# Summing the weighted values of a windowed attention with 32x32 in place of 64x64 identity blocks

## The chip, the cores and the metric

The kernel runs on one core of a Trainium2 chip. The metric is device time in microseconds (us) of one execution, the median of several runs. PE is TensorE (matmuls), PEld its weight loads, DVE is VectorE, ACT is ScalarE, POOL is GpSimd and SP is SyncE, which here only issues transfers. All line numbers (L739) are those of the kernel before.

## The reference

Two independent halves share the inputs' length of S = 2048 tokens and D = 576 channels, and their results stand side by side in the output. Half A is an attention with 32 heads of 18 channels, in which a token sees 8 earlier tokens at a distance of 0, 2, ... 14. Half B is a long convolution. Cut to what matters:

```python
def A(x, wqkv, wo):                  # H = 32, Dh = 18, W = 8, dil = 2
    q, k, v = split(x @ wqkv)
    logits[h, s, w] = q[h, s] . k[h, s - 2 * w] * Dh ** -0.5
    attn = softmax(logits, axis=w)
    o[h, s] = sum_w attn[h, s, w] * v[h, s - 2 * w]      # the change is in this sum
    return o @ wo

def B(q, k, v, shift_k, ssm_k, ssm_D):
    kv = shift(k, shift_k) * v
    return q * (causal_conv(kv, ssm_k) + kv * ssm_D)     # by transforms, written as matmuls

out = concat([A, B], axis=-1)
```

## The kernel before

**Layout.** Half A keeps channels on partitions and time along the free dimension. The 576 channels are four tiles of 128 and one half tile of 64, which is folded so that two halves of the time fill 128 partitions. Time comes in four blocks of 512, each in two halves of 256 (`hh`). A *chunk* `(hh, c)` holds two time blocks for `c` = 0 or 1 (the full tiles), and the folded tile for `c` = 2: six chunks in all.

**Stages.** First come the projections (L310 to L346), the filter spectra of half B (L515 to L530), then the logits (L624, L633), the softmax (L644 to L668), and then the stage of the change, `weigh` (L713 to L758), about 118 to 164 us. Afterwards half B's products (L860), their sums (`ps_z`, L880), the inverse transforms (`ps_inv`, L912, `ps_back`, L953) and the output projection of half A (`ps_wo`, L792) follow.

**weigh.** For a chunk, `spread` (L694) has sent the attention weights to a tile X with each weight repeated for its channels. For a channel tile, DVE multiplies X by the values, shifted by 2, 4, ... 16 places (L723): one instruction of 4096 elements per partition, laid out as two time blocks x 8 window places x 256 tokens. The products P go to three buffers in turn: two wide tiles and a part of `qk`. The sum over the 8 window places is made on PE: matmuls with blocks of the identity matrix as weights, accumulated in PSUM. For `c` < 2 two channel tiles P0 and P1 are summed together (L735 to L741): for each window place, four matmuls of 64x64 with 512 columns, one for each pair of source half and tile. The half `h` of the rows goes to bank `h` and to the half `(h + s) % 2` of the partitions, so that the four use four different blocks of the array. ACT then copies the two banks to `pv` in one instruction (L743). There are eight such sums, four for each `hh`, and two for the folded tile (L753, 256 columns, copied by L757), each of which stands right behind the last of the four.

**Output weights.** As the sum turns one half of the channels, the rows of `wo` are loaded in the order in which the channels lie in `pv` (L765 to L773, on POOL's queue).

**What sets the order.** The program's order is fixed when it is built; at run time each engine works through its list. Between the steps, `until()` (L282) takes as many pieces of independent work from a list `units` as the table `PLACES` says: projections of the values (`ps_proj`), the spectra of half B's input (`ps_fx`, L586, copied by L589), and in the second half the output projection (`ps_wo`, copied by L799). They are put ahead of a sum on PE. A small bookkeeping of clocks (`clk`, `psum`, L258) decides which unit of the inverse transforms is taken in the last stage; the count of pieces doesn't depend on it.

**PSUM.** The pool has two tags, A and B, with two buffers of two banks each (`bank2`, L88). Each request takes the next buffer of its tag, and its first writer waits until the last reader of what was in there is done. `ps_proj`, `ps_wo`, `ps_inv` and `ps_back` use A; the sums (`ps_acc`), the logits and `ps_z` use B; the units of `ps_fx` take B and A in turn (L581), the odd ones B.

Of the kernel before, what the change touches and what calls it, by code (L numbers as in the profile page):

```python
# [11 lines left out]
ACT = mybir.ActivationFunctionType  # L12
# [12 lines left out]
def view(t, offset, dims):  # L25

    return bass.AP(tensor=t.tensor, offset=t.offset + offset, ap=[list(t.ap[0])] + [list(d) for d in dims])
# [3 lines left out]
def kernel(  # L31
# [13 lines left out]
    nc = tc.nc  # L45
    Bsz, S, D = A_x.shape
    assert Bsz == 1 and S == 2048 and D == 576
    H, DH, W, DIL = 32, 18, 8, 2
# [39 lines left out]
    def bank2(name, tag):  # L88
        return pp.tile([128, 2, 512], FP32, name=name, tag=tag)
# [126 lines left out]
    ident = main.tile([128, 128], BF16, name="ident")  # L216
# [18 lines left out]
    for c0, p0, p1 in ((0, 0, 128), (128, 0, 128), (256, 0, 128), (384, 0, 128), (512, 0, 64), (512, 64, 128)):  # L235
        EHS.append(main.tile([128, 32], BF16, name=f"E{len(EHS)}"))
        e = EHS[-1][p0:p1, :]
# [20 lines left out]
    clk = {"D": 0.0, "P": 0.0, "A": 0.0}  # L258
    psum = {"A": deque([0.0, 0.0]), "B": deque([0.0, 0.0])}

    def dve(n, fn, ready=0.0, ns=0.53):

        fn()
        clk["D"] = max(clk["D"], ready) + n * ns / 1000 + 0.125
        return clk["D"]

    def pe(us, tag, evac, ready=0.0, first=True, last=True):

        clk["P"] = max(clk["P"], ready, psum[tag].popleft() if first else 0.0) + us
        clk["A"] = max(clk["A"], clk["P"] + 0.1) + evac  # L270
        if last:
            psum[tag].append(clk["A"])
        return clk["A"]
# [8 lines left out]
    def until():  # L282

        for _ in range(next(places, 0)):
            if units:
                p = max(clk["P"], psum["A"][0] if psum["A"] else 0.0)
                pop(next((n for n, u in enumerate(units) if len(u) < 4 or u[3] <= p), 0))

    def need(label):
        while any(u[2] == label for u in units):  # L290
            pop()
# [141 lines left out]
    for n0 in range(0, D, 256):  # L433
        n = min(256, D - n0)
        ps = bank2("ps_sk", "A" if n == 256 else "B")
        for h in range(0, n, 128):
            w = min(128, n - h)
            sk = skrow[:, 4 * (n0 + h):4 * (n0 + h + w)].rearrange("p (d j) -> p d j", j=4)
            for r in range(2):
                nc.tensor.matmul(ps[64 * r:64 * r + 64, h // 128, 0:4 * w], onesb[:, 0:64],  # L440
                                 sk if r else view(skrow, 4 * (n0 + h) + 3, [[4, w], [-1, 4]]),
                                 start=True, stop=True, tile_position=(0, 64 * r))
# [36 lines left out]
    def taps(i):  # L479
        kj, vt = kjs[i], vts[i]  # L480
        kv = ab[:, i].rearrange("p s c d -> p (s c) d")
        for j in (3, 2, 1, 0):
            o = kv if j == 3 else sp1.tile([128, 4, D], BF16, name="tB")[:]
            dve(2304, lambda: nc.vector.tensor_tensor(  # L484
                o, kj[:, 3 - j:7 - j, :], skb[:, 3 - j, :].unsqueeze(1).to_broadcast([128, 4, D]), ALU.mult))
            if j < 3:
                dve(2304, lambda: nc.vector.tensor_tensor(kv, kv, o, ALU.add))  # L487
        return dve(2304, lambda: nc.vector.tensor_tensor(kv, kv, vt[:], ALU.mult))
# [57 lines left out]
    for i in range(NBL):  # L546
        r = taps(i)
# [51 lines left out]
    for jj, i in ((0, 0), (1, 2)):  # L599
# [6 lines left out]
        for n in range(2):  # L606
            a, b = last[4 * n:4 * n + 4], rest[4 * n:4 * n + 4]
# [4 lines left out]
    def wide(name):  # L612
        return sv.tile([128, 4096], BF16, name=name, tag="prod", bufs=2)
# [69 lines left out]
    pv = main.tile([128, 9216], BF16, name="pv", tag="r_ktok")  # L683
# [29 lines left out]
    def weigh(n):  # L713

        hh, c = chunks[n]
        X = Xt[n]

        def product(ct):
            need(f"v{c}{ct}")
            voff = ct * KW + (1024 * c if ct < 4 else 0)  # L720
            P = qk[:, 8192:12288] if nP[0] % 3 == 2 else wide("P")[:]
            nP[0] += 1
            r = dve(4096, lambda: nc.vector.tensor_tensor(  # L723
                view(P, 0, [[2048, 2], [256, W], [1, 256]]), view(X, 0, [[2048, 2], [256, W], [1, 256]]),
                view(v, voff + 2 + 256 * hh, [[512, 2], [2, W], [1, 256]]), ALU.mult))
            return P, r

        if c < 2:
            for cp in range(2):
                P0, _ = product(2 * cp)  # L730
                yield
                P1, r = product(2 * cp + 1)
                until()
                acc = bank2("ps_acc", "B")
                for u in range(W):  # L735
                    for s, P in enumerate((P0, P1)):
                        for h in range(2):
                            o = (h + s) % 2
                            nc.tensor.matmul(acc[64 * o:64 * o + 64, h, :], ident[64 * h:64 * h + 64, 64 * h:64 * h + 64],  # L739
                                             view(P, 256 * u, [[2048, 2], [1, 256]])[64 * h:64 * h + 64],  # L740
                                             start=(u == 0), stop=(u == W - 1), tile_position=(64 * h, 64 * o))  # L741
                pe(1.9, "B", 1.02, r)
                nc.scalar.activation(view(pv, 4608 * hh + 2048 * c + 1024 * cp, [[512, 2], [1, 512]]), acc[:], ACT.Copy)  # L743
                yield
        else:
            P, r = product(4)
            until()
            acc = bank2("ps_acc", "B")
            for u in range(W):
                for s in range(2):  # L750
                    for h in range(2):
                        o = (h + s) % 2
                        nc.tensor.matmul(acc[64 * o:64 * o + 64, h, 0:256], ident[64 * h:64 * h + 64, 64 * h:64 * h + 64],  # L753
                                         view(P, 2048 * s + 256 * u, [[1, 256]])[64 * h:64 * h + 64],
                                         start=(u == 0), stop=(u == W - 1), tile_position=(64 * h, 64 * o))
            pe(1.0, "B", 0.6, r)
            nc.scalar.activation(view(pv, 4608 * hh + 4096, [[256, 2], [1, 256]]), acc[:, :, 0:256], ACT.Copy)  # L757
            yield  # L758
# [5 lines left out]

    wo = view(qk, 12288, [[2 * D, 2], [D, 2], [1, D]])  # L765
    woh = view(qk, 12288 + 4 * D, [[1, D]])
    for e in range(2):
        for b in range(2):
            nc.gpsimd.dma_start(wo[64 * e:64 * e + 64, :, b, :],
                                bass.AP(tensor=A_wo.tensor, offset=A_wo.offset + ((0, 3), (2, 1))[e][b] * D,  # L770
                                        ap=[[9 * D, 64], [4 * D, 2], [1, D]]))
        nc.gpsimd.dma_start(woh[64 * e:64 * e + 64, :],
                            bass.AP(tensor=A_wo.tensor, offset=A_wo.offset + 8 * D, ap=[[9 * D, 64], [1, D]]))  # L773
    nst = [0]
# [31 lines left out]
    def outputs(hh):  # L806
        for j in range(2):
            for sb in (2 * hh, 2 * hh + 1):
                for h in range(2):
                    units.append((1.15, partial(output, j, sb, h), "wo"))  # L810

    pvs = (None for n in range(len(chunks)) for _ in weigh(n))
    steps(pvs, 1)
    steps(sb_, 1)
# [50 lines left out]
    acc = {}  # L865

    def sums(j, t, i, pr, ready):

        until()
        sc, ss = CSG[j - i], SSG[j - i]  # L870
        for r, terms in enumerate((((0, 0, sc), (1, 1, ss)), ((1, 0, sc), (0, 1, -ss)))):
            if i == 0:
                acc[r] = bank2("ps_z", "B")
                clk["P"] = max(clk["P"], psum["B"][r])
            for n, (part, cs, sign) in enumerate(terms):
                w = ident if sign > 0 else identn
                for s in range(2):
                    for h in range(2):
                        o = 64 * ((h + s) % 2)
                        nc.tensor.matmul(view(acc[r], 512 * h, [[192, 2], [96, 2], [1, 96]])[o:o + 64], w[64 * h:64 * h + 64, 64 * h:64 * h + 64],  # L880
                                         pr[64 * h:64 * h + 64, part, cs, :].rearrange(
                                             "p (a g e) -> p g a e", a=2, g=4)[:, 2 * s:2 * s + 2],
                                         start=(i == 0 and n == 0), stop=(i == j and n == 1),
                                         tile_position=(64 * h, o))
            clk["P"] = max(clk["P"], ready) + 0.34
        if i == j:
            for r in range(2):
                y, z = (view(Yall, (j % 2) * 8 * D + r * 4 * D + TH * t, [[2 * D, 2], [D, 2], [1, TH]]),
                        view(acc[r], 0, [[512, 2], [TH, 2], [1, TH]]))
                if (j, t, r) == (NBL - 1, 2, 1):  # L890
                    nc.vector.tensor_copy(y, z)
                else:
                    nc.scalar.activation(y, z, ACT.Copy)  # L893
                out = pe(0.0, "B", 0.85)
            return out
# [102 lines left out]
    for n, (j, t, i) in enumerate(todo):  # L998
# [3 lines left out]
        r = sums(j, t, i, *prs.pop(n))  # L1002
        new = []
        if i == j and t == 2 and j < NBL - 1:
            a, b = inverse(j, 0, HD, r), inverse(j, HD, HD, r)
# [40 lines left out]
```

## Time and profile before

| what | us |
|---|---|
| median of 3 runs (224.27 to 224.85) | 224.3 |
| the profiled execution | 225.0 |
| its span on the core | 223.0 |
| PE busy, share of the span | 213.1, 96% |
| DVE busy | 208.1, 93% |
| ACT busy | 154.4, 69% |
| granted TensorE clock | full throughout |

"Busy" counts the time in which at least one instruction of the engine runs; matmuls overlap, so a busy PE isn't a PE at its peak. A group's row gives the line, engine and operation, what it writes and reads, the shape, the count, its busy time and the mean of one, then the idle time of the engine before it and what ended that. A row of the timeline gives the start and the length in us, and a group may hold several instructions of one line in a row. A row of the windows gives the length of the stretch, the busy time of PE, PEld, DVE, ACT and POOL, each with its count, then the granted clock, the share of the transfer engines and GB/s.

### The profile page before, as it was taken

To read this page: it belongs to the slowest core of one execution; us is meant where nothing else is said; L and a number is where in the kernel's file an instruction comes from. 1 tells how busy PE (TensorE), PEld (TensorE's weight loads), DVE (VectorE), ACT (ScalarE), POOL (GpSimd) and SP (SyncE) were. 2 spreads that over 40 slices of the span, in tenths; PEclk is the share of its full clock that TensorE was granted. 3 is DMA by queue.
4 is the path that set the end of the run, shared out by engine and by line. 5 is a ranking of instruction groups with operands and counts; after the bars stand their busy time and mean duration, and the time that the engine had idled before them with its cause. 6 is when DMAs were issued, how large, how long until landed. Compare 5 with 4: busy or idle time off the path is not lost.

```text
span 223.0 us, 5309 instructions
## 1 busy us (share of the span) xinstructions
PE 213.1 (96%) x2271; PEld 118.2 (53%) x2271; DVE 208.1 (93%) x156; ACT 154.4 (69%) x213; POOL 31.9 (14%) x68
## 2 busy tenths in 40 slices
PE   7999999999999999999999999999999999999891
PEld 2543444444566556753444445665656667666560
DVE  7789999999988999999899999999999899999992
ACT  5858766888596987756667768885678887655630
POOL 8860000000000040403410000015000000330000
PEclk9999999999999999999999999999999999999999
DMA  5999999999900047659999469917211103662016
GB/s 187 274 229 219 188 241 203 221 207 235 216 0 0 3 83 131 117 95 169 198 190 235 124 114 203 225 32 234 88 56 53 57 3 107 199 208 75 3 53 159
DMA packets 30985, 31.41 MB, mean 141 GB/s; under 512 B 16849, under 2 KB 26705, under 8 KB 30962
## 3 DMA queue, kind: packets, MB, share of 16 engines
q1 hardware_dynamic: 25714, 21.93, 44.6%
q0 software_dynamic: 2624, 6.64, 14.6%
q10 hardware_dynamic: 2624, 2.51, 3.3%
q8 instruction: 17, 0.28, 0.5%
q14 instruction: 6, 0.05, 0.1%
HBM read 13.11 MB, written 4.72 MB: 80 GB/s over the span
## 4 chain that ended last, share of the span: by engine, by line
PE 76%; DVE 9%; ACT 5%; issue 4%; DMA 3%; SPq 1%; DVEq 0%; ACTq 0%
PE ps_proj L310 15%; PE ps_fk L515 10%; PE ps_wo L792 7%; PE ps_fx L586 6%; DVE qk L860 6%; PE ps_z L880 5%; PE ps_log L633 5%; PE ps_fk L516 5%; PE ps_acc L739 4%; PE ps_inv L912 4%; PE ps_proj L427 3%; PE ps_proj L315 3%; DMA X<-attn 3%; PE ps_proj L322 3%; PE ps_idle L138 2%
## 5 line engine op out<-in xcount | busy, mean ns | idle before, releaser
L860 DVE TENSOR_TENSOR qk<-xw,Ks 128x3072 bf16<-128x3072 bf16 x30 | 50.5, 1750 | 1.2 <-PE ps_z L880 1.0
L624 DVE TENSOR_TENSOR prod<-qk 128x4096 bf16<-128x4096 bf16 (+1 forms) x20 | 40.6, 2074 | 3.4 <-PE ps_log L633 3.3
L310 PE MATMUL ps_proj<-xw 128*128 128x512 bf16 x160 | 38.4, 380 | 0.0
L515 PE MATMUL ps_fk<-kTok,TK 128*128 128x384 bf16 x128 | 32.8, 327 | 0.6 <-ACT Ks L530 0.5
L516 PE MATMUL ps_fk<-kTok,TK 128*128 128x192 bf16 x128 | 31.4, 246 | 0.0
L530 ACT ACTIVATE Ks<-ps_fk 128x576 bf16<-128x576 f32 x32 | 20.4, 653 | 9.9 <-PE ps_fk L516 9.7
L310 PEld LDWEIGHTS <-xw 128*128 128x128 bf16 x160 | 14.3, 98 | 18.9 <-issue 4.9
L893 ACT ACTIVATE Yall<-ps_z 128x768 bf16<-128x768 f32 x23 | 17.4, 808 | 6.1 <-PE ps_z L880 5.9
L346 ACT ACTIVATE qk<-ps_proj 128x1024 bf16<-128x1024 f32 x14 | 14.4, 1027 | 7.1 <-PE ps_proj L310 3.4
L589 ACT ACTIVATE xw<-ps_fx 128x576 bf16<-128x576 f32 x32 | 18.6, 660 | 0.2
L515 PEld LDWEIGHTS <-TK 128*128 128x128 bf16 x128 | 12.5, 98 | 11.8 <-issue 4.2
L792 PE MATMUL ps_wo<-qk,pv 128*128 128x288 bf16 x128 | 17.9, 287 | 0.0
L586 PE MATMUL ps_fx<-ab,TX 64*128 64x288 bf16 x256 | 17.7, 283 | 0.0
L487 DVE TENSOR_TENSOR ab<-ab,tB 128x2304 bf16<-128x2304 bf16 x12 | 16.3, 1358 | 0.4
L880 PE MATMUL ps_z<-qk,ident 64*64 64x384 bf16 x288 | 16.4, 325 | 0.3 <-ACT pv L743 0.3
L484 DVE TENSOR_TENSOR tB<-kj,skb 128x2304 bf16<-128x2304 bf16 x12 | 16.3, 1356 | 0.3
L912 PE MATMUL ps_inv<-Yall,TI 128*128 128x288 bf16 (+1 forms) x112 | 15.5, 292 | 0.7 <-ACT Yall L893 0.6
L739 PE MATMUL ps_acc<-P,ident 64*64 64x512 bf16 x192 | 15.3, 379 | 0.0
L346 ACT ACTIVATE v<-ps_proj 128x1024 bf16<-128x1024 f32 x9 | 9.2, 1022 | 8.8 <-PE ps_proj L322 4.6
L586 PEld LDWEIGHTS <-TX 64*128 64x128 bf16 x256 | 11.7, 94 | 6.5 <-issue 3.6
L799 ACT ACTIVATE qk<-ps_wo 128x576 bf16<-128x576 f32 x16 | 10.4, 651 | 6.1 <-PE ps_wo L792 3.0
L792 PEld LDWEIGHTS <-pv 128*128 128x128 bf16 x128 | 11.5, 98 | 6.0 <-issue 3.2
(146 smaller groups left out, 352.8 us busy)
## 6 DMA issues: line engine op xcount, KB each, us to landing
kj<-in_B_k_dram SPq DMA_DIRECT2D x7, 504.0 KB, 8.1
Ks<-Ks POOLq DMA_DIRECT2D x6, 576.0 KB, 7.7
qk<-attn SPq DMA_DIRECT2D x12, 256.0 KB, 5.8
vt<-in_B_v_dram SPq DMA_DIRECT2D x8, 288.0 KB, 8.6
out_dram<-qk ACTq DMA_DIRECT2D x8, 288.0 KB, 2.9
X<-attn SPq DMA_DIRECT2D x8, 256.0 KB, 5.1
Ks<-in_A_x_dram SPq DMA_DIRECT2D x2, 576.0 KB, 5.2
xw<-in_A_wqkv_dram SPq DMA_DIRECT2D x2, 576.0 KB, 7.4
```

The source lines that it names most:

```text
L310: nc.tensor.matmul(ps[:, jp, :], wq(kb, comp, 128 * ct, 128), xT(kb, 1024 * jj + 512 * jp, 512), start=(kb == 0 and not first), stop=(kb = ...
L346: nc.scalar.activation(view(t, o + pad + 1024 * jj, [[512, 2], [1, 512]]), ps[:], ACT.Copy)
L515: nc.tensor.matmul(o[:, 0:2], w, rhs[:, 0:2], start=start, stop=stop)
L516: nc.tensor.matmul(o[:, 2], w, rhs[:, 2], start=start, stop=stop)
L530: nc.scalar.activation(view(Ks, (3 - m) * SPB + 4 * D * cs + 96 * gi, [[768, 3], [384, 2], [1, 96]]), acc3(ps), ACT.Copy, scale=(CSG, SSG) ...
L586: nc.tensor.matmul(ps[:, pm, 0:HD], TX[64 * pm:64 * pm + 64, c, 128 * gi:128 * gi + 128], kv[64 * pm:64 * pm + 64, c, HD * h:HD * h + HD], ...
L624: r = dve(1024 * nj, lambda: nc.vector.tensor_tensor(view(prod, 0, [[256 * nj, 4], [256, nj], [1, 256]]), view(t, o + 256 * hh, [[0, 4], [ ...
L739: nc.tensor.matmul(acc[64 * o:64 * o + 64, h, :], ident[64 * h:64 * h + 64, 64 * h:64 * h + 64], view(P, 256 * u, [[2048, 2], [1, 256]])[6 ...
L792: nc.tensor.matmul(ps[:, r, 0:HD], oT(hh, j + 2 * r, t)[:, o:o + 128], wo[:, t // 2, t % 2, HD * h:HD * h + HD], start=(t == 0 and h == 0) ...
L860: r = dve(3072, lambda: nc.vector.tensor_tensor(pr, view(xw, i * SPB + 4 * TH * t, [[4 * D, 2], [0, 2], [1, 4 * TH]]), view(Ks, (3 - j + i ...
L880: nc.tensor.matmul(view(acc[r], 512 * h, [[192, 2], [96, 2], [1, 96]])[o:o + 64], w[64 * h:64 * h + 64, 64 * h:64 * h + 64], pr[64 * h:64 ...
L912: nc.tensor.matmul(ps[:, c, 0:n], TI[:, sl, pm, 128 * c:128 * c + 128], Yall[:, j % 2, pm, sl, c0:c0 + n], start=(pm == 0 and sl == 0), st ...
```

## The change

For `c` < 2 the sum is made with 32x32 blocks of the identity: for each window place sixteen matmuls of 256 columns, for the two channel tiles `p`, the two time blocks `jj` and the four groups `g` of 32 rows. The group goes to the partitions `32 * ((g + p + 2 * jj) % 4)`, and each pair `(p, jj)` has a PSUM bank of its own, so that a sum takes four banks: both buffers of tag B. ACT copies them out in three instructions: the first time block's two banks (128 partitions), and the second time block's in two pieces of 64 partitions, which swap the halves of the partitions so that both time blocks lie alike in `pv`. As the second channel tile of a pair is turned by 32 partitions there, the rows of the output weights are loaded in five pieces in place of four. The folded tile's sum stays as it was. The bookkeeping of clocks gets the new figures.

```diff
@@ weigh, c < 2
-                acc = bank2("ps_acc", "B")
+                acc = [bank2("ps_acc", "B") for _ in range(2)]
                 for u in range(W):
-                    for s, P in enumerate((P0, P1)):
-                        for h in range(2):
-                            o = (h + s) % 2
-                            nc.tensor.matmul(acc[64 * o:64 * o + 64, h, :], ident[64 * h:64 * h + 64, 64 * h:64 * h + 64],
-                                             view(P, 256 * u, [[2048, 2], [1, 256]])[64 * h:64 * h + 64],
-                                             start=(u == 0), stop=(u == W - 1), tile_position=(64 * h, 64 * o))
-                pe(1.9, "B", 1.02, r)
-                nc.scalar.activation(view(pv, 4608 * hh + 2048 * c + 1024 * cp, [[512, 2], [1, 512]]), acc[:], ACT.Copy)
+                    for p, P in enumerate((P0, P1)):
+                        for jj in range(2):
+                            for g in range(4):
+                                o = 32 * ((g + p + 2 * jj) % 4)
+                                nc.tensor.matmul(acc[jj][o:o + 32, p, 0:256], ident[32 * g:32 * g + 32, 32 * g:32 * g + 32],
+                                                 view(P, 2048 * jj + 256 * u, [[1, 256]])[32 * g:32 * g + 32],
+                                                 start=(u == 0), stop=(u == W - 1), tile_position=(32 * g, o))
+                to = view(pv, 4608 * hh + 2048 * c + 1024 * cp, [[512, 2], [256, 2], [1, 256]])
+                clk["P"] = max(clk["P"], psum["B"][1])
+                pe(1.0, "B", 0.6, r)
+                nc.scalar.activation(to[:, :, 0], acc[0][:, :, 0:256], ACT.Copy)
+                pe(0.0, "B", 1.2, r)
+                for e in range(2):
+                    nc.scalar.activation(to[64 * e:64 * e + 64, :, 1], acc[1][64 - 64 * e:128 - 64 * e, :, 0:256], ACT.Copy)
                 yield
@@ output weights
+    for b, c, n, p, i in ((0, 0, 64, 0, 0), (0, 1, 64, 64, 0), (1, 2, 64, 32, 0), (1, 3, 32, 96, 0), (1, 3, 32, 0, 32)):
+        nc.gpsimd.dma_start(wo[p:p + n, :, b, :], bass.AP(tensor=A_wo.tensor, offset=A_wo.offset + (9 * i + c) * D,
+                                                          ap=[[9 * D, n], [4 * D, 2], [1, D]]))
     for e in range(2):
-        for b in range(2):
-            nc.gpsimd.dma_start(wo[64 * e:64 * e + 64, :, b, :],
-                                bass.AP(tensor=A_wo.tensor, offset=A_wo.offset + ((0, 3), (2, 1))[e][b] * D,
-                                        ap=[[9 * D, 64], [4 * D, 2], [1, D]]))
         nc.gpsimd.dma_start(woh[64 * e:64 * e + 64, :],
                             bass.AP(tensor=A_wo.tensor, offset=A_wo.offset + 8 * D, ap=[[9 * D, 64], [1, D]]))
```

## The prediction

> **What bounds the kernel now.** I read the page first, then the windows and the timeline of the stage that the change is in (the weighted values, 118 to 164 us), then the rows of ps_acc.
>
> ```profile
> PE 213.1 (96%) x2271; PEld 118.2 (53%) x2271; DVE 208.1 (93%) x156; ACT 154.4 (69%) x213; POOL 31.9 (14%) x68
> ...
> q8 instruction: 17, 0.28, 0.5%
> ...
> L860 DVE TENSOR_TENSOR qk<-xw,Ks 128x3072 bf16<-128x3072 bf16 x30 | 50.5, 1750 | 1.2 <-PE ps_z L880 1.0
> ```
>
> PE and DVE are both nearly full. Stage by stage (columns: length, then PE, PEld, DVE and ACT busy, clock) neither has room here, and ACT has little in the middle:
>
> ```profile
> 134.00:138.00 4.00, 4.00 (x70) 2.56 (x70) 3.90 (x2) 3.08 (x6) 0.00 (x0) 1.00 0.93 202
> ...
> 142.00:146.00 4.00, 4.00 (x69) 2.90 (x69) 4.00 (x3) 4.00 (x8) 0.00 (x0) 1.00 0.80 210
> ```
>
> So a shorter sum on PE can win only what DVE still idles behind PE: after 118 us that is one wait of 1.04 us (at 176.7, in the 1.2 above) and two of 0.1. The ceiling of the gain is about 1.2 us. The floor is a question of what the sum waits for. The first sum, in order of time:
>
> ```profile
> 119.65 1.91 ACT L658 ACTIVATE attn<-attn 128x2048 bf16<-128x2048 bf16 x1 [0.58 <-ACT v L346]
> ...
> 119.99 1.14 PE L586 MATMUL ps_fx<-ab,TX 64*128 64x288 bf16 x16
> ...
> 121.06 1.92 PE L739 MATMUL ps_acc<-P,ident 64*64 64x512 bf16 x32
> 121.47 1.00 ACT L346 ACTIVATE v<-ps_proj 128x1024 bf16<-128x1024 f32 x1
> ...
> 122.38 1.18 ACT L589 ACTIVATE xw<-ps_fx 128x576 bf16<-128x576 f32 x2
> ```
>
> The reader is to see that PE starts the sum at 121.06 while the two ps_fx units just before it are still in PSUM: ACT copies them only from 122.38. That is no harm today, as the sum takes one of the two B buffers and the odd unit (ps_fx takes B, A, B, A in turn) holds the other. That B is a ring is seen at 163.73, where ps_z waits for the sum's copy:
>
> ```profile
> 163.73 0.84 PE L880 MATMUL ps_z<-qk,ident 64*64 64x384 bf16 x12 [0.25 <-ACT pv L743]
> ```
>
> **The change, part by part.**
>
> *The sums on PE.* Before, a round is four matmuls of 512 columns that start together, and rounds start 0.215 us apart: 8 rounds and the step to the next unit make 1.85 us (121.06 to 122.92). After, a round is sixteen of 256 columns. L753, in the rows of ps_acc below (durations min/median/max in ns, then first and last start), has 256-column rounds 0.109 apart and takes 1.00 us (140.53 to 141.53).
>
> ```profile
> L753 PE MATMUL ps_acc<-qk,ident x64: 269/269/293, 140.5 to 163.2; 64*64 64x256 bf16 x64
> L743 ACT ACTIVATE pv<-ps_acc x8: 1024/1024/1035, 123.4 to 162.7; 128x1024 bf16<-128x1024 f32 x8
> L757 ACT ACTIVATE pv<-ps_acc x2: 592/595/598, 141.7 to 163.6; 128x512 bf16<-128x512 f32 x2
> ```
>
> In the trace a weight load with its matmul starts every 3.4 ns, so sixteen pairs need 0.054 us, less than a round's 0.109. I take 1.02 us a sum, a gain of 0.83, 6.6 in all eight. No row has sixteen blocks at once. From above, if they serialise by four, a sum takes 8 x 4 x 0.109 + 0.15 = 3.6; by eight, 1.85; from below 0.95.
>
> Do four row blocks into one bank run together? Each (p, jj) sends four row groups to one bank, in different partitions. The nearest rows do that with two:
>
> ```profile
> 207.09 0.29 PE L953 MATMUL ps_back<-yA,flip 64*64 64x288 bf16 x4
> ...
> 207.21 0.29 PE L953 MATMUL ps_back<-yA,flipn 64*64 64x288 bf16 x4
> ```
>
> L953 writes each bank from both row halves, and four such matmuls start every 0.12 us (288 columns): no serialising, so I keep 1.02. The Trainium skill (TensorEngine Tiling (Array Packing), Restrictions and Gotchas) states that different row tiles cannot access the same PSUM bank at once. By that rule a sum would take 3.6 us; the L953 rows contradict it where the partitions differ.
>
> *The new wait.* The sum's fifth matmul writes the second tile, and PE runs in order, so each sum now starts when both B buffers are empty: behind the copy of the last odd ps_fx unit. Behind it in PE's queue stands everything. ACT's rows, back to back: L346 0.92 a copy, L589 0.54 (the last one 0.65), a 128x512 copy 0.50 (the last 0.595). No row has a copy of 64 partitions or one that moves partitions; I take L757's price, bounds 0.40 to 0.60. A sum's three copies then hold ACT for 1.6 us (1.02 before), and the first B buffer is free 0.6 after the sum's end, the second 1.6.
>
> Now I carry PE's delay against the trace through the eight sums, in their order: the trace's start of each, when B is empty, and then PE's delay on arrival, its wait, and its delay at the unit behind. That last one is arrival plus wait less the 0.83 that the shorter sum gives back. What ACT and PE do between two sums keeps its order and its row durations.
>
> 1. 121.06: ps_fx copied until 123.03, so 123.08. Arrives at 0, waits 2.0, leaves at +1.2.
> 2. 129.37: the last odd unit's copy (129.42 to 130.07 in the trace) comes 1.25 later, 131.32. Arrives +1.2, waits 0.8, leaves +1.2.
> 3. 133.97: proj copy 133.49 + 1.18, then 0.92 and 0.65 for the ps_fx unit: 136.25. Arrives +1.2, waits 1.2, leaves +1.5.
> 4. 138.38: the sum ends 137.3; ACT does three copies (1.5), then four ps_fx units (3 x 0.54 + 0.65): 141.13. ps_fx itself waits 0.3 for the copies. Arrives +1.8, waits 1.05, leaves +2.0. L753 follows at once and needs the first copy: it waits 0.8 and leaves +2.5 (0.2 of wait for DVE in the trace is gone).
> 5. 145.11: L757's copy, then seven ps_fx units (6 x 0.54 + 0.65) from 144.69: 148.6. Arrives +2.5, waits 1.2, leaves +2.7.
> 6. 149.52: as 4. Arrives +3.0, waits 1.05, leaves +3.2.
> 7. and 8. 153.89, 160.69: only ps_wo (A) is between, ACT is done in time. Leaves +2.4, then +1.5. L753 behind sum 8 waits 0.8 for its copy, and ps_z for L753's: +2.4 when ps_z's first unit ends.
>
> In total: waits of 7.3 at sums 1 to 6, 1.5 at the two L753 (with a step of 0.09 each for the new change of block size), 0.5 at ps_z and 0.55 at ps_fx, together 9.9; less 6.6; less 0.9 that PE waits in the trace at these places (0.5 at ps_z for B, the rest for DVE) and then no longer does: **+2.4 us on PE at 164 us.** The same steps with the old durations give the eight starts of the trace within 0.1 us.
>
> *DVE.* A product writes one of three buffers in turn, so it needs the sum that read the product three before it, and the trace has them meet within 0.1 us (sum 2 ends 131.29, the next product starts 131.40). So the sums' later ends push DVE: 1.0 at that one, 1.4 two products on, +3.1 at L860's start (160.41). There DVE idled 1.04 at 176.7 and 0.1 at 172.3, for PE; of this PE's +2.4 leaves 0.35. From then on DVE is full up to the end, so both arrive at **+2.4**.
>
> *Copies on ACT* beyond those waits: eight times 0.6 us, in gaps. *Output weights:* five loads in place of four on POOL at 0.63 each, same bytes, issued 109 to 112 and landed in some 14 us, needed at 151.4: hidden with 25 us to spare, cost nothing. *The planner:* its clocks decide only which inverse unit is taken later; bound 0.5 either way, I take 0.
>
> *Instructions.* q8 moved 0.28 MB for 4542 PE instructions, 62 bytes each; a new sum is 256 instructions, one of q8's packets (0.28 MB / 17 = 16 KB), in 0.95 us. A packet took 0.005 x 16 x 223 / 17 = 1.05 us. If fetching lags, it costs 0 to 1.05 us a sum. PE stands still before six of the sums, which gives it time: I take 0.
>
> The sum: 225.0 (profiled run: span 223.0 and 2.0 around it) + 2.4 = 227.4. That run lies 0.7 above the median of the three, 224.3; on the median it is **226.7**.
>
> **The rivals.** *Faster: the second B buffer is free in time.* The place is ACT's order before each sum. For it: no ps_acc row waits for ACT today. The price: without waits at sums 1 to 7, PE is 1.2 ahead at ps_z, and DVE's idle 1.1 goes: 223.2. It decides from the point where the waits shrink by 0.35 us at each of seven places. Against: 122.38 in the timeline and 4.00 of 4.00 on ACT. Chance 0.10.
>
> *Blocks serialise.* By eight, a sum is 1.85 as before and the waits stay: +9, 233; by four +23, 247. For: no row has four row groups. Against: L953, and L633 with four column groups at once. Chance 0.08.
>
> The Trainium skill (TensorE: Matmul & The Clock Gate, Part 3) reports sixteen 32x32 tiles at 10.6 times one; no row here shows it.
>
> *Fetching lags.* The place is inside each sum. 0.4 us there adds at all eight (3.2, with none of it hidden by DVE): +5.6, 229.9; with a whole packet's time at each, +10.8. Chance 0.14.
>
> *No difference:* the waits come out a third shorter and balance the gain, within 0.7 us. Chance 0.11.
>
> **How the numbers follow.** The forecast has 0.57, its own range 225.2 (copies at 0.40: +1.6, and a sum of 0.95: 0.6 less) to 228.4 (copies at 0.60: +3.2, and a sum of 1.1: 0.9 more). About 0.3% is what a measurement can tell from no change. Faster 0.10, same 0.11, slower 0.79. The range 223.8 to 230.0 leaves out the serial blocks and most of the faster case.
>
> **What would show it.** After: PE ps_acc waits for ACT xw (L589) before sums 1 to 6, 2 us at the first; sixteen starts within 0.06 us, rounds 0.11 apart, about 1.0 us a sum; L753 waits for the first copy; DVE waits for PE ps_acc at products, and little at 176. Wrong if ps_acc waits for nothing, if rounds are over 0.15 apart, or if PE sits on issue inside a sum.

## The result and the profile after

The changed kernel takes 239.25 us (median; 237.34 to 240.2), the kernel before 224.57 us on the same chip: a ratio of 1.0635 [1.0554, 1.0716]. The forecast was 226.7. The direction was right; the size, 14.7 in place of 2.4 us, lies far outside the range. Executions of one kernel differ with the granted clock (the changed kernel's four took 240.0, 240.2, 238.5 and 237.3 us at mean clocks of 0.974, 0.982, 0.982 and 0.993; the profile is of the first), and those over 1.5% above the fastest of their kernel are left out of the ratios: two of the third experiment's four, its profiled one among them.

The profiled execution took 240.0 us, its span 238.2. In this kernel the sum's matmul is L740, the first copy L746, the two others L749; L753 is now L759, and L880 is L885. Its page, answering to the lines shown of before:

```profile
PE 214.9 (90%) x3029; PEld 123.2 (52%) x3039; DVE 208.4 (88%) x156; ACT 161.3 (68%) x229; POOL 32.3 (14%) x69
...
PEclk9999999999999999999999995599999999999998
...
q8 instruction: 23, 0.38, 0.7%
...
L723 DVE TENSOR_TENSOR P<-X,v 128x4096 bf16<-128x4096 bf16 x6 | 13.6, 2288 | 9.4 <-PE ps_acc L740 9.4
...
L740 PEld LDWEIGHTS <-ident 32*32 32x32 bf16 x1024 | 10.0, 89 | 11.1 <-issue 10.1
```

PE is busy for about as long as before, in a longer span. The products of DVE (L723) idle 9.4 us for the sums. PE itself idles on "issue": it waits for nothing that the profile shows. The clock row has two slices at half, and q8 (packets, MB, share of the transfer engines) brings 23 packets where it brought 17.

The first sum, in the timeline of PE (start, length, then in brackets the idle time before it):

```profile
120.86 0.29 PE L740 MATMUL ps_acc<-P,ident 32*32 32x256 bf16 x4
122.86 1.41 PE L740 MATMUL ps_acc<-P,ident 32*32 32x256 bf16 x124 [1.71 <-ACT xw L589]
```

This is the forecast's new wait: four matmuls into the first buffer, then a stand until ACT has emptied the second, 2.0 us from start to start. Later the same view shows something else, ahead of and inside sum 4:

```profile
138.05 1.39 PE L586 MATMUL ps_fx<-ab,TX 64*128 64x288 bf16 x15
142.87 2.24 PE L586 MATMUL ps_fx<-ab,TX 64*128 64x288 bf16 x25 [3.42 <-issue]
145.04 1.71 PE L740 MATMUL ps_acc<-P,ident 32*32 32x256 bf16 x103
148.24 0.63 PE L740 MATMUL ps_acc<-P,ident 32*32 32x256 bf16 x25 [1.49 <-issue]
149.56 0.85 PE L759 MATMUL ps_acc<-qk,ident 64*64 64x256 bf16 x11 [0.70 <-ACT pv L746]
```

PE stops within a run of ps_fx matmuls and within a sum, where no operand is missing. In the windows (length, PE, PEld, DVE, ACT, POOL, clock, transfer share, GB/s) the clock follows:

```profile
138.00:142.00 4.00, 1.36 (x29) 0.73 (x16) 3.86 (x2) 2.43 (x4) 0.00 (x0) 1.00 0.63 141
142.00:146.00 4.00, 3.13 (x104) 2.39 (x103) 0.64 (x1) 2.38 (x4) 0.00 (x0) 0.75 0.95 215
146.00:150.00 4.00, 1.81 (x91) 1.20 (x75) 1.14 (x1) 1.06 (x2) 0.00 (x0) 0.50 0.15 42
150.00:154.00 4.00, 4.00 (x50) 2.66 (x44) 4.00 (x3) 2.40 (x5) 0.00 (x0) 0.50 0.00 0
```

The same stretch before, where PE was busy 3.77 to 4.00 of each 4 us from 134 to 150:

```profile
138.00:142.00 4.00, 3.77 (x80) 2.16 (x78) 4.00 (x3) 3.08 (x6) 0.00 (x0) 1.00 0.97 218
```

After the change PE is busy 1.36 there, and behind the stop the granted clock is halved, from 144.0 to 154.2. What DVE pays, in its timeline:

```profile
148.86 4.49 DVE L723 TENSOR_TENSOR P<-X,v 128x4096 bf16<-128x4096 bf16 x2 [6.22 <-PE ps_acc L740]
...
158.71 2.29 DVE L723 TENSOR_TENSOR P<-X,v 128x4096 bf16<-128x4096 bf16 x1 [3.15 <-PE ps_acc L740]
```

**Where the stops are.** I put the rows of PE and PEld in order of their starts and counted them. There are five stops of PE without a releaser from 118 to 180 us, before the instructions 2743, 2999, 3511, 3767 and 4023 of that count: 3.71, 1.88, 1.33, 0.43 and 1.29 us from start to start, 8.6 together. These counts are all 183 above a multiple of 256. (The trace lacks some ten matmul rows ahead of this stage, 3029 matmuls to 3039 loads, so it is the constancy of the remainder that counts and not its value.) A packet of q8 has 16,384 bytes, and 23 packets for the 6068 PE instructions here (17 for 4542 before) make some 265 instructions a packet: the remainder says 256. The packet records in the trace complete it, here for three of the five stops:

| PE uses up a block | the packet for the block after the next starts | ends | its first instruction runs | PE had run out of the next block at |
|---|---|---|---|---|
| 136.75 | 140.56 | 141.53 | 142.87 | 139.16 |
| 142.87 | 145.71 | 146.99 | 148.24 | 146.36 |
| 161.10 | 162.20 | 163.14 | 164.56 | 164.13 |

So PE holds about two blocks of 256 instructions, and a packet comes only once a block has been used up. From that to the first instruction of the new block it takes 3.5 us in the third row, where hardly anything else is transferred, and 6.1 and 5.4 in the first two, where the transfer share is 0.9 and more. A new sum alone is a whole block, and with the units beside it PE gets through a block in 2.4 us (136.75 to 139.16). In the kernel before, PE took some 7 us for its fastest block of the stage, so that a block had that long to arrive, and there is no such stop.

**The account.** PE from the first sum's start to ps_z: 42.7 us before (121.06 to 163.73), 57.7 after (120.86 to 178.55), 15.0 more, as much as the whole execution (240.0 less 225.0). By terms, in us:

| term | forecast | measured |
|---|---|---|
| eight sums, shorter by 0.83 each; measured 1.34 in place of 1.85, so 0.51 | -6.6 | -4.1 |
| waits for a B buffer at sums 1 to 6 (1.99, 0.74, 1.12, 0, 1.01, 0.41) | +7.3 | +5.3 |
| waits of L753 for the first copy (0.77, 0.72) | +1.5 | +1.5 |
| stops for instructions | 0 | +8.6 |
| half clock, 144.0 to 154.2: what the stretches from sum 3's end to sum 5 took beyond their undisturbed durations, the waits and the stops (0.73, 0.54, 0.86, 1.31) | 0 | +3.4 |
| the rest (forecast: ps_z, ps_fx, old waits) | +0.2 | +0.3, left over |

The half clock's term is that of this execution; the one with a mean clock of 0.993 took 2.7 us less, which fits it.

### The profile page after: what moved, and what is told of

The parts are those of the page before. It is cut to its first block, busy times and chain, and to the rows that moved or that the text cites. A ratio compares the mean times of both kernels' runs of the same rounds, so it can differ in the third digit from the quotient of the medians.

```text
span 238.2 us, 6853 instructions
## 1 busy us (share of the span) xinstructions
PE 214.9 (90%) x3029; PEld 123.2 (52%) x3039; DVE 208.4 (88%) x156; ACT 161.3 (68%) x229; POOL 32.3 (14%) x69
## 4 chain that ended last, share of the span: by engine, by line
PE 62%; DVE 11%; ACT 10%; issue 9%; DMA 3%; SPq 2%; DVEq 0%; ACTq 0%
PE ps_proj L310 11%; PE ps_fk L515 7%; PE ps_wo L797 6%; PE ps_acc L740 5%; DVE qk L865 5%; PE ps_z L885 5%; PE ps_inv L917 3%; PE ps_fk L516 3%; PE ps_fx L586 3%; DMA pv<-attn 3%; ACT xw L589 3%; PE ps_log L633 2%; PE ps_proj L427 2%; DVE prod L624 2%; SPq L701 2%
## 5 line engine op out<-in xcount | busy, mean ns | idle before, releaser
L310 PE MATMUL ps_proj<-xw 128*128 128x512 bf16 x151 | 37.0, 380 | 0.8 <-issue 0.6
L586 PE MATMUL ps_fx<-ab,TX 64*128 64x288 bf16 x256 | 20.4, 302 | 4.6 <-issue 4.5
L589 ACT ACTIVATE xw<-ps_fx 128x576 bf16<-128x576 f32 x32 | 19.2, 653 | 4.3 <-PE ps_fx L586 4.0
L723 DVE TENSOR_TENSOR P<-X,v 128x4096 bf16<-128x4096 bf16 x6 | 13.6, 2288 | 9.4 <-PE ps_acc L740 9.4
L586 PEld LDWEIGHTS <-TX 64*128 64x128 bf16 x256 | 12.9, 100 | 12.1 <-issue 8.5
L740 PE MATMUL ps_acc<-P,ident 32*32 32x256 bf16 x768 | 13.4, 294 | 5.8 <-ACT xw L589 3.3
L885 PE MATMUL ps_z<-qk,ident 64*64 64x384 bf16 x288 | 16.6, 325 | 0.3
L740 PEld LDWEIGHTS <-ident 32*32 32x32 bf16 x1024 | 10.0, 89 | 11.1 <-issue 10.1
L854 POOL DMA_DIRECT2D qB<-in_B_q_dram x4 | 2.9, 731 | 93.9 <-DVE P L723 48.6
```

The costliest lines, as they stand in the source:

```text
L310: nc.tensor.matmul(ps[:, jp, :], wq(kb, comp, 128 * ct, 128), xT(kb, 1024 * jj + 512 * jp, 512), start=(kb == 0 and not first), stop=(kb = ...
L586: nc.tensor.matmul(ps[:, pm, 0:HD], TX[64 * pm:64 * pm + 64, c, 128 * gi:128 * gi + 128], kv[64 * pm:64 * pm + 64, c, HD * h:HD * h + HD], ...
L589: nc.scalar.activation(view(xw, SPB * i + 96 * gi + 1152 * h, [[4 * D, 2], [384, 3], [1, 96]]), view(ps, 0, [[512, 2], [96, 3], [1, 96]]), ...
L740: nc.tensor.matmul(acc[jj][o:o + 32, p, 0:256], ident[32 * g:32 * g + 32, 32 * g:32 * g + 32], view(P, 2048 * jj + 256 * u, [[1, 256]])[32 ...
```

## The experiments

The theory: the forecast's waits for the B buffers are there and are worth a few us; the remainder is the supply of PE's instructions, in blocks of 256, with the half clock as its echo. The rivals: the waits alone, grown by pushing one another; the 32x32 blocks themselves, slowed when four row groups write one bank; the transfers. The ratios are against the kernel before on the same chip.

**1. The buffers alone.** The kernel before, its sum's two banks taken one from each B buffer, so that two copies follow. Its 64 PE instructions a sum stay.

```diff
-                acc = bank2("ps_acc", "B")
+                acc = [bank2("ps_acc", "B") for _ in range(2)]
...
-                            nc.tensor.matmul(acc[64 * o:64 * o + 64, h, :], ...
+                            nc.tensor.matmul(acc[h][64 * o:64 * o + 64, 0, :], ...
...
+                for h in range(2):
+                    nc.scalar.activation(view(pv, 4608 * hh + 2048 * c + 1024 * cp + 512 * h, [[1, 512]]), acc[h][:, 0, :], ACT.Copy)
```

> The sums stay as before (64x64 blocks, 64 instructions), but their two banks are taken from both B buffers, with two copies: the new wait alone, without the shorter sum and without more instructions. Theory (the wait for B costs what the prediction's steps gave, and the rest of the loss is the supply of PE's instructions): no pause of PE over 0.5 us without a releaser; each sum waits for ps_fx's copy, and since nothing is given back the same steps give +8.0 us: 232.3. Rival (the waits and copies make up the whole loss of 14.7 us, which is after a gain of some 5): at least +18, 242 or more.

Measured: 232.35 us against 225.43, ratio 1.0316 [1.0261, 1.0371]. From the rows of its sum, what ended PE's idle time before it:

```profile
  ACT xw L589: 3.8, 6
```

From start to start the six waits are 1.99, 0.75, 1.13, 0.60, 1.09 and 0.60, and L753's counterpart waits 1.06 and 1.07: 8.3, less the 0.9 of old waits 7.4, where the time grew by 6.9. No stop of over 0.4 us is without a releaser. So the step "The new wait" holds by itself, and with no gain on PE to set against it, it costs 6.9 us.

**2. The instructions alone.** The kernel before with one B buffer and one copy, each of its matmuls cut into four of 128 columns: 256 PE instructions a sum, with 64x64 blocks.

```diff
+                    for n in range(4):
...
-                                             view(P, 256 * u, [[2048, 2], [1, 256]])[64 * h:64 * h + 64],
...
+                                                 view(P, 2048 * (n // 2) + 256 * u + 128 * (n % 2), [[1, 128]])[64 * h:64 * h + 64],
```

> The kernel before with each matmul of a sum cut into four of 128 columns: 256 instructions a sum, as many as after, with the old blocks, one B buffer and one copy. Theory (supply of instructions): PE pauses of 0.4 to 4 us, each at a whole number of 256 instructions and 1.2 to 1.5 us behind the end of a q8 packet; a sum itself 1.85 to 2.2 us; +7 us (from +4 to +12): 231. Rival (waits for B): no pauses, within 1.5 us of the kernel before.

Measured: 232.86 us, ratio 1.032 [1.0261, 1.0378]. An undisturbed sum takes 1.91 us (1.85 before), and no sum waits for a B buffer. In PE's timeline, and in a window of 1 us:

```profile
135.82 0.90 PE L586 MATMUL ps_fx<-ab,TX 64*128 64x288 bf16 x12
138.70 2.08 PE L586 MATMUL ps_fx<-ab,TX 64*128 64x288 bf16 x24 [1.98 <-issue]
140.71 3.14 PE L740 MATMUL ps_acc<-P,ident 64*64 64x128 bf16 x128
```

```profile
140.00:141.00 1.00, 1.00 (x20) 0.45 (x19) 0.22 (x1) 0.79 (x3) 0.00 (x0) 0.50 0.94 307
```

Four stops, at the counts 2743, 3511, 3767 and 4023 (2.26, 0.64, 0.45, 0.52 us): the same counts as in the changed kernel, with other blocks, other buffers and another copy. Behind the first the clock is halved, and sum 4 takes 3.1 us. The same columns through the same blocks in four times the instructions cost 7.4 us. Some 0.5 of it are the longer sums (8 x 0.06); the remainder is the missing term without the new wait. (The profiled execution, 231.1 us, is the fastest of four.)

**3. The waits alone taken away.** The changed kernel with all ps_fx units in tag A, so that B belongs to the sums.

```diff
-            tag = filler_tag("fx", "AB")
+            tag = filler_tag("fx", "A")
```

> The changed kernel with all ps_fx units in tag A: the sums no longer wait for ps_fx's copies. Theory: the waits before sums (5.3 us in the changed kernel's profile) go, the pauses at blocks of 256 instructions stay or grow, since the same instructions are wanted sooner; 2 to 5 us faster than the changed kernel: 234 to 237. Rival (waits for B are the loss): 226 or less.

Measured: a ratio of 1.0545 [1.0472, 1.0618], 237.2 to 238.0 us. That is just above the 234 to 237 that were expected, and the interval overlaps that of the changed kernel. From the profile I read the order of the waits and no sizes. The sums no longer wait for ps_fx, but the ps_fx units wait for their predecessors and for ps_proj in the two A buffers. The edit moved the wait and did not remove it. It can't tell what the waits are worth; that is left to the first experiment. The stops stand at the counts 2487, 2743, 2999, 3511 and 4023 here: another pattern of waits, and the same remainder of 183. (At 2743 the profile names ACT as the releaser, but there too the packet had ended only 1.3 us before.)

**4. Supply without competition.** The changed kernel without the transfers that spread the last three chunks' weights: these chunks are computed with other weights, and part of the output is left out.

```diff
-    spread(3)
-    spread(4)
+    for n, X in ((3, X0[:]), (4, qk[:, 4096:8192]), (5, qk[:, 0:4096])):
+        Xt[n] = X
...
-    spread(5)
```

> The changed kernel without the transfers of the attention weights of the last three chunks (these chunks are computed with other weights, so that part of the output is left out): the transfer engines are nearly idle from 124 us on. Theory: a q8 packet starts about 1.1 us after PE has used up a block, in place of 2.3 to 3.8, so the pauses at 139 and 146 us (3.7 and 1.9) shrink to under 1.5 each and the granted clock stays full; the pauses in quiet stretches stay; 4 to 7 us faster than the changed kernel: 232 to 235. Rival (the pauses have nothing to do with transfers): within 1 us of the changed kernel, 238 to 240.

Measured: 234.49 us, ratio 1.0409 [1.0356, 1.0461]. The same stretch, timeline and windows:

```profile
138.33 1.39 PE L586 MATMUL ps_fx<-ab,TX 64*128 64x288 bf16 x15
140.66 1.75 PE L586 MATMUL ps_fx<-ab,TX 64*128 64x288 bf16 x25 [0.93 <-issue]
142.34 1.60 PE L740 MATMUL ps_acc<-P,ident 32*32 32x256 bf16 x103
144.11 0.41 PE L740 MATMUL ps_acc<-P,ident 32*32 32x256 bf16 x25 [0.17 <-issue]
```

```profile
138.00:142.00 4.00, 2.98 (x81) 2.19 (x63) 3.57 (x2) 3.46 (x6) 0.00 (x0) 1.00 0.01 4
```

The stops stand behind the same 15th matmul and the same 103rd; they are 1.22 and 0.43 us in place of 3.71 and 1.88, and the clock stays full. With a transfer share of 0.01, the packets for these two blocks start 0.9 and 1.1 us after a block is used up, in place of 3.8 and 2.8. Beside the transfers that remain, at 158.7, it is 2.5 again, and the stop behind it 1.57. So these transfers make up some 5 us of the loss (1.0635 less 1.0409, of 225), the halved clock with it, and 9 us remain without them.

**5. The blocks alone.** 32x32 blocks with 512 columns into one B buffer, one copy, the output weights loaded as in the change: four row groups write each bank, 128 instructions a sum.

```diff
+                    for p, P in enumerate((P0, P1)):
+                        for g in range(4):
+                            o = 32 * ((g + p) % 4)
+                            nc.tensor.matmul(acc[o:o + 32, p, :], ident[32 * g:32 * g + 32, 32 * g:32 * g + 32],
+                                             view(P, 256 * u, [[2048, 2], [1, 256]])[32 * g:32 * g + 32],
...
```

> 32x32 blocks with 512 columns: eight blocks at once, 128 instructions a sum, one B buffer, one copy, the turned output weights as in the changed kernel. Theory (supply: about 3.5 us for 256 instructions while transfers are light, 5 to 6 while they are heavy): a sum takes about 1.9 us as before, at most one or two pauses of under 1 us, and the time lies within 1.5 us of the kernel before: 224 to 226. Rival (32x32 blocks as such, or four row groups writing one bank, are slow): rounds over 0.25 us apart, +4 us or more.

Measured: 224.64 us against 225.26, ratio 0.9983 [0.9966, 1.0001]. The rows of its sum:

```profile
L739 PE MATMUL ps_acc<-P,ident x384: 371/374/386, 120.5 to 162.0; 32*32 32x512 bf16 x192
```

Rounds of eight start 0.216 us apart and a sum takes 1.85 us, as with four 64x64 blocks: eight run together, four of them into one bank. The forecast's rival "Blocks serialise" falls, and the row loads of the output weights cost nothing that shows. The one stop, 0.59 us at the count 2487 (183 above a multiple of 256 again), suggests that 128 instructions a sum are about what the supply bears.

**6. The forecast's waits with few instructions.** The changed kernel with four of the eight window places in each sum, so that half of the weighted values are left out: its buffers and copies, 128 instructions a sum.

```diff
-                for u in range(W):
+                for u in range(W // 2):
```

> The changed kernel with four of the eight window places in its sums (half of the weighted values are left out): 128 instructions a sum, still both B buffers and three copies. Theory: a sum takes 0.85 us from its release, the waits for B stay (2.0 before the first), pauses of PE are gone or under 1 us; the prediction's steps with 0.85 in place of 1.02 give +1 on PE and +2 on DVE: 225.5 to 227.5. Rival (the loss is in the waits and copies, which are all here): 232 or more.

Measured: 226.57 us, ratio 1.0088 [1.0054, 1.0122]. From the rows of ps_acc:

```profile
L759 PE MATMUL ps_acc<-qk,ident x64: 266/269/293, 141.5 to 164.7; 64*64 64x256 bf16 x64
...
  ACT xw L589: 5.3, 6
```

All six of the forecast's waits are there, from start to start 1.98, 0.74, 1.12, 1.02, 1.07 and 1.02 (forecast 2.0, 0.8, 1.2, 1.05, 1.2, 1.05). No stop of over 0.4 us is without a releaser; a wait of 0.79 us at a unit of ps_wo is for ACT's copy of an earlier unit. With the supply out of the way, the waits come as the forecast carried them, within 0.13 each. In the changed kernel those at sums 4 and 6 are smaller because the stops give ACT time.

**7. The same work at other counts.** The changed kernel with 64 matmuls of one column at its start, 128 PE instructions more.

```diff
+    ps = bank2("ps_idle", "A")
+    for _ in range(64):
+        nc.tensor.matmul(ps[:, 0, 0:1], zeros[:, 0:128], zeros[:, 0:1], start=True, stop=True)
```

> The changed kernel with 64 one-column matmuls more at its start, while PE waits for the first transfers: every later instruction of PE moves by 128, half a block. Theory: the pauses stay at the same counts modulo 256 of PE's instructions, so they come 128 instructions earlier in the program than in the changed kernel, and the time moves by at most 4 us either way. Rival (the pauses belong to places in the program, as the reading of a certain tile): they stay at their places, at the same units as in the changed kernel.

Measured: 235.9 us, ratio 1.0488 [1.0433, 1.0543]. The first stop, in PE's timeline (ps_fx is L589 here):

```profile
128.22 0.91 PE L589 MATMUL ps_fx<-ab,TX 64*128 64x288 bf16 x12
130.57 0.42 PE L589 MATMUL ps_fx<-ab,TX 64*128 64x288 bf16 x4 [1.44 <-issue]
```

The stops have moved to other places in the work (before sum 2, and three later), but the counts are 2231, 3254, 4022 and 4278, again 182 or 183 above a multiple of 256. They sum to 3.9 us in place of 8.6 (1.72, 0.73, 0.86, 0.60), the clock stays full, and the time is 3.3 us less (1.0635 less 1.0488, of 225), although the first sum starts 1.9 us later. The count of instructions decides where PE can stop; how fast the work there uses a block up and what else is transferred decide whether it does, and for how long.

**8. One sum only.** The fifth kernel with only the seventh sum as in the change, where the change has no wait before it.

```diff
+                if (hh, c, cp) == (1, 1, 0):
...
+                else:
+                    acc = bank2("ps_acc", "B")
```

> Seven of the eight sums as with 32x32 blocks of 512 columns (128 instructions, one B buffer), and only the seventh as in the changed kernel (256 instructions, both B buffers, three copies): in front of it stand only units of ps_wo, which use A, so it waits for no copy, and PE is late behind it. Theory: that sum takes 1.35 us in place of 1.9, PE comes 0.5 us sooner to the eighth sum, DVE's idle of 1.04 at 176.6 us shrinks to 0.5, and the time is 0.3 to 0.6 us under that of 32x32 blocks of 512 columns (224.6), if no boundary of 256 instructions gives a pause there: 224.1. Rival (a lone sum of 256 instructions already outruns the supply): a pause of 1 us or more in or behind it and 225 or more.

Measured: 224.65 us against 225.32, ratio 0.9973 [0.9951, 0.9995]. The sum by itself, in the timeline:

```profile
154.19 0.30 PE L741 MATMUL ps_acc<-P,ident 32*32 32x256 bf16 x8
...
154.31 0.29 PE L741 MATMUL ps_acc<-P,ident 32*32 32x256 bf16 x8
...
154.50 0.33 PE L741 MATMUL ps_acc<-P,ident 32*32 32x256 bf16 x8
...
154.63 0.33 PE L741 MATMUL ps_acc<-P,ident 32*32 32x256 bf16 x8
...
155.57 1.15 PE L809 MATMUL ps_wo<-qk,pv 128*128 128x288 bf16 x8
```

No stop and no wait, and still 1.38 us and not 1.02: the first two rounds start 0.12 apart, later ones 0.13 to 0.19. DVE's idle time behind ps_z is 1.02 us as before, so the 0.47 us that this sum saves never reached the end. The expected 0.3 to 0.6 us under the fifth kernel did not come: the ratios are 0.2 us apart, and their intervals overlap. No version beat the kernel before by more than 0.3%.

## Why the prediction was wrong in size

**The step that failed** is "Instructions": "If fetching lags, it costs 0 to 1.05 us a sum. PE stands still before six of the sums, which gives it time: I take 0." Three things were wrong in it. The price: I took a packet's own time on its queue, 1.05 us, for the price of supply. That is about a third of it or less; before it the packet waits 1.0 to 3.8 us at the five stops, and after it 1.25 to 1.42 us pass until PE runs. The cover: PE's stands before sums are 2 us or less, where a block needs 3.5 to 6.1 from the use of one to the first instruction of another. The unit: I counted by the sum, but supply goes by count, so the first two stops fell into ps_fx units and into the middle of a sum. The second experiment puts the step's price at 7.4 us in the kernel before; in the changed kernel it is the 8.6 + 3.4 us of the account. The half clock follows the first stop, of 3.71 us; where the stops are 1.72 us and less (fourth, fifth and seventh), it stays full.

**The sum on PE**, 1.02 forecast, is 1.34. I read 3.4 ns between pairs where PE had a queue of them ready. In the changed kernel's trace the pairs start 8.3 ns apart once the first 64 or so queued instructions are gone: 16 x 8.3 = 0.133 us, more than the 0.109 in which the array takes 256 columns. That makes 2.6 us over the eight sums. My own steps with 1.34 us give +5.0.

**The new wait** was right in place and mechanism, and in size where nothing else disturbs it (sixth experiment, and 2.0 us at the first sum of the changed kernel). The waits of L753 were forecast at 0.8 and are 0.77 and 0.72. Two waits were written larger than the forecast's own times give: sum 5 arrives at 147.6 and finds B empty at 148.65, so 1.05 in place of 1.2 (1.07 measured), and sum 3 1.13 in place of 1.2 (1.12). The forecast's delays behind these sums go by the smaller ones.

**The copies.** I took 0.595 for a copy of 64 partitions, between 0.40 and 0.60. The rows give the price, and the upper bound was near:

```profile
L749 ACT ACTIVATE pv<-ps_acc x16: 588/591/595, 124.9 to 177.9; 64x512 bf16<-64x512 f32 x16
L746 ACT ACTIVATE pv<-ps_acc x8: 597/597/597, 124.3 to 176.7; 128x512 bf16<-128x512 f32 x8
```

**Blocks into one bank**: right, by the fifth experiment. The forecast kept the L953 rows against the Trainium skill's rule (TensorEngine Tiling (Array Packing), Restrictions and Gotchas), and eight 32x32 matmuls, four into each bank, in 0.216 us show the rule not to hold where the partitions differ.

**DVE**: forecast to take up the same +2.4. It idled 14.0 us for sums in all (2.2, 6.2, 3.2, 1.8, 0.6 at five products) and keeps its 1.0 us behind ps_z, as PE is late all the way. **Output weights**: nothing, as forecast.

**The rivals.** "Fetching lags" named the mechanism, its place inside the sums and its sign, at a chance of 0.14, with +10.8 as its upper price. It should have been the forecast: the page before showed 62 bytes an instruction and packets of 256, and the change adds 1536 instructions to 43 us of a full PE. The question that I did not put to the trace was how long PE takes for 256 instructions there, and how long a packet takes from the use of a block to the first instruction. In the kernel before, a packet is never late, so the second number has only a bound there; that alone called for a range up to the 10.8. Even this price was too small: it has 8.4 us for the supply, a packet's time in each sum, where the stops and the half clock took 12.0.

What stays open: why a block's first instruction runs 1.25 us or more after its packet has ended, what exactly the packet waits for while transfers are dense, and why the pairs beyond the first 64 instructions come 8.3 ns apart.

## What to carry to other kernels

Before a matmul is cut into smaller ones, count the instructions per microsecond: here PE's instructions (a matmul and its weight load are two) came in blocks of 256. Where PE stood for one, it came 3.2 to 4.0 us after a block was used up while few transfers ran, and 4.2 to 6.1 us beside dense ones (a share of 0.8 and more), so that a stretch that uses them faster stops. Stops without a releaser at a constant remainder of 256 are the sign of it, and a long one is paid for again by the clock. A buffer that is taken twice as wide is priced by the last reader before it, and that part can be carried by hand to 0.1 us.

## What the runs showed of the hardware

- **Supply of instructions.** Packets of 16,384 bytes; a stop of 0.43 to 3.71 us where 256 instructions are used faster than the next come. The Trainium skill (Runtime: NRT & Kernel Launch, Instruction fetch mechanics) has the refill in blocks of 16 KiB, 256 instructions, which the counts bear out; it calls the cost of crossing a block mostly hidden, and in the changed kernel 8.6 us of it were not.
- **Clock.** Stops of 3.71 us (changed kernel) and of 2.26 us (second experiment) were followed, 1.1 us behind their ends, by a granted clock of 0.50 for some 10 and 3 us; stops of 1.72 us and less in the fourth, fifth and seventh experiments were not. In the third experiment's profile a stop of 1.15 and a wait of 0.81 us close together stand ahead of a second stretch at 0.50, so that no run gives the least length. The Trainium skill (TensorE: Matmul & The Clock Gate, Part 1) gives an idle window of about 3.4 us for it; the stop of 2.26 us, within 2 us of which the clock was at 0.50, is shorter than that, and the measurement decides.
- **Pairs.** A 32x32 weight load with its matmul starts every 3.4 ns out of a full queue and every 8.3 ns beyond it.
- **Copies.** ACT takes 0.59 us for 64 partitions that move to the other half as for 128 that stay (0.60), with 512 elements each.
